# Four KV pairs per round in 32 KB rows, and zero descriptors of 56 KB, in a gradient kernel that writes 280 MB

## The chip, the cores and the metric

The kernel runs on one core of one Trainium2 chip. The metric is the device time of one execution in microseconds (us). The profile is of one execution on the same core; its times start at the span's first instruction.

## The reference, cut to what matters

The kernel computes a gated attention step and its gradients. One token of each of two batches (B = 2) attends to the last W = 4096 positions of a cache of 32768, with 32 query heads on 8 KV heads (4 query heads each) of width 128, all in bfloat16:

```python
q = xn @ wq                        # per head
s = q k_win^T / sqrt(128);  p = softmax(s);  o = p v_win
out = x + (o @ wo) * silu(mlp(xn))
# gradients wanted: x, k_cache, v_cache, wq, wo, w1, b1, w2, b2
dv_win = p^T do;   ds = p * (do v_win^T - delta);   dk_win = ds^T q
```

The gradients of the K and V caches have the caches' full shape, [2, 8, 32768, 128] each. Only the window of 4096 rows of each of the 32 (tensor, batch, head) slabs is not zero. So of 268 MB of cache gradient 235 MB are zeros that have to be written, 33.6 MB are computed, and 33.6 MB of K and V are read.

## The kernel before

**Zero fill.** A tile `zt` of zero bytes (L77) is the source of all zero writes. `zf` (L87 to L94) issues one DMA on the GpSimd queue (q0 in the profile) that reads bytes and writes bfloat16: one byte of `zt` becomes two bytes in memory. With `ZG = 112` rows of 256 bytes a descriptor writes 28 KB, and a slab of 28672 zero rows is 256 descriptors in one DMA. Five slabs are cut by hand (`zshort`) into DMAs of odd shapes. The fills are issued ahead of everything else in program order and run through the whole kernel. The last slab is written at the very end by a DMA on SyncE's queue (L616), which waits for the fill before the last one.

**Prologue.** Small vectors come in on ScalarE's queue (q10): `x`, `grad_out`, `b1`, `b2` (L195 to L201). The weights come in on SyncE's queue (q1): `w1`, `w2`, `wo`, `wq` (L203 to L207). Layernorm, the MLP, q and do are computed; the buffers of this stage lie in a pool `pw` whose memory the attention stage uses again.

**Attention, eight rounds.** A round is one KV head `hk` of both batches. K and V are tiles of 128 partitions by 64 blocks of 128; the even partitions hold batch 0 and the odd ones batch 1, each partition 64 consecutive cache rows (16 KB). A tile is loaded by two DMAs of 1 MB on SyncE's queue (L347) and stored by two on ScalarE's queue (L407). Four tiles of 16 KB per partition rotate (`kvp`, `bufs=4`), so that the next round's loads can be in flight. A round does:

- `scores` of K (L372 transposes, L145/L143 copies out of PSUM, L377 matmuls), then the softmax;
- `scores` of V with do, `contract` of V with p (L392), which gives o, and ds;
- `outer_store` of V: p^T do overwrites the V tile in place (L402 matmuls, copied by ScalarE and VectorE) and is stored;
- `contract` of K with ds, `outer_store` of K, and the round's share of dx and of the gradient of wq (L469 to L485).

The program is written in that order; a planner that works with its own costs and the program's order as priority fixes the order on each engine. On TensorE it puts transposes of the next round's K between the outer products of this round's V.

**Epilogue.** After the rounds the pool's memory goes to the epilogue's tiles. `o_rows` (L496) is the first of them; then come the projection by wo, the MLP's gradients (`dw_st`, stored at L603 and L611), the last zero slab (L616), and the gradient of wo (L621, stored at L623 on ScalarE's queue).

Of the kernel before, what the change touches and what calls it, by code (L numbers as in the profile page):

```python
# [8 lines left out]
ACT = mybir.ActivationFunctionType  # L9
ALU = mybir.AluOpType  # L10
# [6 lines left out]
def kernel(  # L17
# [37 lines left out]
    PB = P // B  # L55
    NCB = W // PB
    CC = NCB // G
    RB = G * REP
    R = B * RB
# [3 lines left out]
    assert B == 2 and REP == 4 and NCB == 64 and DH == P and RB == 32 and CW == 512  # L63
# [12 lines left out]
    ZG = 112  # L76
    zt = const.tile([P, ZG * DH], mybir.dt.uint8, name="zt")  # L77
# [9 lines left out]
    def zf(o, q, r0, nent, rows, rep=1):  # L87
        b, hk = divmod(q, HKV)
        nr = nent * rows * rep
        v = o[b, hk, r0:r0 + nr, :].rearrange("(r p g) d -> p r (g d)", p=nent, g=rows)  # L90
        st = 4 if nent < 16 else 1
        zs = zt[0:nent * st:st, 0:rows * DH].unsqueeze(1).to_broadcast([nent, rep, rows * DH])
        sw_fill.append(nc.gpsimd.dma_start(out=v, in_=zs))  # L93
        return r0 + nr  # L94
# [6 lines left out]
        4: ((3, 1, 2), (2, 99, 6), (128, 112, 1), (128, 102, 1), (86, 1, 1)),  # L101
        6: ((3, 1, 2), (3, 106, 2), (128, 112, 1), (128, 106, 1), (126, 1, 1)),
        8: ((4, 96, 6), (128, 112, 1), (128, 94, 1)),
        10: ((4, 69, 2), (128, 112, 1), (128, 107, 1), (88, 1, 1)),
# [29 lines left out]
    acc_dxn = const.tile([B, D], F32, name="acc_dxn")  # L134
# [35 lines left out]
    nc.vector.tensor_reduce(out=m8[:], in_=ident_bf[0:R, 0:R].rearrange("p (b g i) -> p g b i", b=B, i=REP), axis=AX.XY, op=ALU.add)  # L170
# [6 lines left out]
    NZ = 2  # L177
    ZO = R - REP
    zq_bufs, zdo_bufs, p_bufs = [], [], []
    for j in range(NZ):  # L180
        t = const.tile([P, B, ZO + R], BF16, name=f"zq{j}")
        nc.vector.memset(t[:], 0.0)
        zq_bufs.append(t)
        t = const.tile([P, B, ZO + R], BF16, name=f"zdo{j}")
        nc.vector.memset(t[:], 0.0)
        zdo_bufs.append(t)
        t = const.tile([R, CC, PB, B], BF16, name=f"p{j}")
        nc.vector.memset(t[:], 0.0)
        p_bufs.append(t)
    ds_bf = const.tile([R, CC, PB, B], BF16, name="ds_bf")  # L190
# [137 lines left out]
    kvp = attn.enter_context(tc.tile_pool(name="kvp", bufs=4))  # L328
    kvt = attn.enter_context(tc.tile_pool(name="kvt", bufs=4))
    wsl = attn.enter_context(tc.tile_pool(name="wsl", bufs=1))  # L330
    small = attn.enter_context(tc.tile_pool(name="small", bufs=2))
    hkp = attn.enter_context(tc.tile_pool(name="hkp", bufs=2))
    one = attn.enter_context(tc.tile_pool(name="one", bufs=1))
    bdp = attn.enter_context(tc.tile_pool(name="bdp", bufs=1))

    kwin = slice(SK - W, SK)
    kvs = {}

    def rows_of(t, b, hk):
        return t[b, hk, kwin, :].rearrange("(p c) d -> p c d", c=NCB)  # L340

    def load_kv(hk):
        tiles = []
        for src in (A_k_cache, A_v_cache):
            nat = kvp.tile([P, NCB, DH], BF16, tag="nat")
            for b in range(B):
                dma_load.dma_start(out=nat[b:P:B], in_=rows_of(src, b, hk))  # L347
            tiles.append(nat)
        kvs[hk] = tiles
# [7 lines left out]
    def block_diag(hT, tag):  # L357
        zr = small.tile([P, B, G, REP], BF16, tag="zr" + tag)
        for b in range(B):
            nc.vector.tensor_copy(out=zr[:, b], in_=hT[:, :, b].unsqueeze(1).to_broadcast([P, G, REP]))  # L360
        rp = ps_m.tile([R, P], F32, tag="m")
        nc.tensor.matmul(rp[:], lhsT=zr[:].rearrange("p b g i -> p (b g i)"), rhs=ident_bf[:, :], start=True, stop=True)  # L362
        bd = bdp.tile([R, G, DH], BF16, tag="bd" + tag)
        nc.vector.tensor_tensor(out=bd[:], in0=rp[:].unsqueeze(1).to_broadcast([R, G, DH]),  # L364
                                in1=m8[:].unsqueeze(2).to_broadcast([R, G, DH]), op=ALU.mult)
        return bd

    def scores(out_ps, nat, zbuf):
        for g in range(G):
            tp = ps_t.tile([P, CC, P], BF16, tag="pt")  # L370
            for j in range(CC):
                nc.tensor.transpose(tp[:, j, :], nat[:, g * CC + j, :], ident_bf[:, :])  # L372
            tT = kvt.tile([P, CC, PB, B], BF16, tag="tT")
            evac(tT[:].rearrange("p c k b -> p (c k b)"), tp[:].rearrange("p c k -> p (c k)"), eng=("act" if g % 4 == 3 else "dve"))
            for b in range(B):
                o = ZO - (b * RB + REP * g)
                nc.tensor.matmul(out_ps[:], lhsT=zbuf[:, b, o:o + R], rhs=tT[:, :, :, b],  # L377
                                 start=(g == 0 and b == 0), stop=(g == G - 1 and b == B - 1))

    def col_form(src, tag):  # L380
        tp = ps_m.tile([P, CC, R], BF16, tag="m")
        for cc in range(CC):
            nc.tensor.transpose(tp[:, cc, :], src[:, cc].rearrange("r k b -> r (k b)"), ident_bf[0:R, 0:R])
        t = one.tile([P, CC, B, G, REP], BF16, tag="colT")
        nc.vector.tensor_copy(out=t[:].rearrange("p c b g i -> p c (b g i)"), in_=tp[:])  # L385
        return t

    def contract(nat, tT):
        ps = ps_m.tile([P, B, REP], F32, tag="m")
        for c in range(NCB):  # L390
            g, cc = divmod(c, CC)
            nc.tensor.matmul(ps[:], lhsT=nat[:, c, :], rhs=tT[:, cc, :, g, :],  # L392
                             start=(c == 0), stop=(c == NCB - 1))
        return ps

    def outer_store(src, bd, nat, dst, hk):
# [9 lines left out]
        for b in range(B):  # L406
            dma_store.dma_start(out=rows_of(dst, b, hk), in_=nat[b:P:B])  # L407

    load_kv(0)
    for hk in range(HKV):  # L410
        if hk + 1 < HKV:
            load_kv(hk + 1)
        knat, vnat = kvs.pop(hk)
        hs = slice(hk * REP, (hk + 1) * REP)
        zq, zdo, p_bf = (t[hk % NZ] for t in (zq_bufs, zdo_bufs, p_bufs))
        nc.vector.tensor_copy(out=zq[:, :, ZO:ZO + REP], in_=qT_all[:, hs, :].rearrange("p i b -> p b i"))
        nc.vector.tensor_copy(out=zdo[:, :, ZO:ZO + REP], in_=doT_all[:, hs, :].rearrange("p i b -> p b i"))
        dqT_bf = hkp.tile([P, REP, B], BF16, tag="dqT_bf")
# [15 lines left out]
        for b in range(B):  # L434
            rb = slice(b * RB, (b + 1) * RB)
            nc.scalar.activation(out=p_bf[rb, :, :, b], in_=e_sb[rb], func=ACT.Copy, scale=rl[rb, 0:1])
# [3 lines left out]
        pT = col_form(p_bf, "pT")  # L440
        o_ps = contract(vnat, pT)
        nc.vector.tensor_copy(out=oT_all[:, hs, :].rearrange("p i b -> p b i"), in_=o_ps[:])

        junk = one.tile([R, CC, PB], BF16, tag="junk")
        dpp = small.tile([R, 1], F32, tag="dpp")
        dp_c = dp_ps[:].rearrange("r (c k) -> r c k", c=CC)
        nc.vector.scalar_tensor_tensor(out=junk[:], in0=dp_c, scalar=rl[:, 0:1], in1=e_sb[:],
# [3 lines left out]
        for b in range(B):  # L451
            rb = slice(b * RB, (b + 1) * RB)
            nc.vector.scalar_tensor_tensor(out=ds_bf[rb, :, :, b], in0=dp_c[rb], scalar=delta[rb, 0:1], in1=p_bf[rb, :, :, b],
                                           op0=ALU.subtract, op1=ALU.mult)
        bddo = block_diag(doT_all[:, hs, :], "do")
        outer_store(p_bf, bddo, vnat, out_3, hk)
        dsT = col_form(ds_bf, "dsT")
        dq_ps = contract(knat, dsT)
        nc.scalar.mul(out=dqT_bf[:].rearrange("p i b -> p b i"), in_=dq_ps[:], mul=SCALE)
        bdq = block_diag(qT_all[:, hs, :], "q")  # L460
        outer_store(ds_bf, bdq, knat, out_2, hk)

        wqT = wsl.tile([P, REP, DK, P], BF16, tag="wqT")
        for half in range(2):
            tp = ps_t.tile([P, 8, P], BF16, tag="pt")
            for jj in range(8):
                i, k = divmod(half * 8 + jj, DK)
                n0 = (hk * REP + i) * DH
                nc.tensor.transpose(tp[:, jj, :], wq[:, k, n0:n0 + DH], ident_bf[:, :])  # L469
            evac(wqT[:, half * 2:(half + 1) * 2, :, :].rearrange("q i k p -> q (i k p)"), tp[:].rearrange("q a p -> q (a p)"))  # L470
        xps = ps_m.tile([B, DK, P], F32, tag="m")
        for i in range(REP):
            nc.tensor.matmul(xps[:], lhsT=dqT_bf[:, i, :], rhs=wqT[:, i, :, :], start=(i == 0), stop=(i == REP - 1))
        if hk == 0:
# [4 lines left out]
        for i in range(REP):  # L479
            nc.tensor.transpose(tp[:, i, :], dqT_bf[:, i, :], ident_bf[:, :])  # L480
# [170 lines left out]
```

## Time and profile before

| | |
|---|---|
| median of 3 runs | 769.88 us (769.7 to 770.0) |
| the profiled execution: its own time, and its span | 769.5 us, 767.7 us |
| TensorE matmul, VectorE, ScalarE busy | 468.0, 283.4, 212.0 us |
| moved by the DMA queues | 326.68 MB, mean 426 GB/s |
| of it by q0 (GpSimd: fills), q1 (SyncE), q10 (ScalarE) | 227.55, 56.63, 41.95 MB |
| DMA packets | 17016, of which 3109 under 512 B |

The page has the span in 40 slices of 19.2 us. A line "DMA" gives the busy share of the 16 DMA engines in tenths, a line "GB/s" what they moved. A DMA answer for a stretch of time gives for each queue the packets, the MB and the time that its packets took as a share of 16 engines. In a timeline the bracket at the end of a line is the time for which the engine sat idle before, and what it waited for.

### The profile page before, as it was taken

What the parts mean: (1) busy time and instruction counts of PE and PEld (TensorE: products, weight loads), DVE (VectorE), ACT (ScalarE), POOL (GpSimd) and SP (SyncE); (2) the same over time, 40 slices, a digit from 0 to 9 for tenths busy, and PEclk for the clock granted to TensorE, in tenths of its full rate; (3) what the DMA queues carried; (4) which work ended last, traced back from release to release, by engine and by line L of the source; (5) the groups of instructions that cost most, each with busy time, mean ns of one, the idle gap of its engine ahead of it and who ended that gap; (6) DMA issues with size and microseconds to landing.
All of it is one profiled execution on the core that took longest, in us unless ns stands there. A gap on an engine that the chain in (4) does not pass through costs nothing.

```text
span 767.7 us, 8822 instructions
## 1 busy us (share of the span) xinstructions
PE 468.0 (61%) x3778; PEld 233.6 (30%) x3778; DVE 283.4 (37%) x546; ACT 212.0 (28%) x325; POOL 31.9 (4%) x55
## 2 busy tenths in 40 slices
PE   0166752898498498479569749959884266850000
PEld 0153341444244234233324413433441234210000
DVE  3033331465255255245325415434553034740000
ACT  0034440345135135224324313323442100530000
POOL 3000001010000010000000000000000000000000
PEclk9997885979859759758857955675985565555555
DMA  9999999999999999999999999999999999999998
GB/s 358 432 431 421 437 430 426 427 429 428 431 426 429 427 430 426 431 431 423 429 434 429 424 433 429 425 434 426 428 432 430 432 429 433 429 428 436 432 429 348
DMA packets 17016, 326.68 MB, mean 426 GB/s; under 512 B 3109, under 2 KB 3118, under 8 KB 3128
## 3 DMA queue, kind: packets, MB, share of 16 engines
q0 software_dynamic: 9728, 227.55, 70.0%
q1 hardware_dynamic: 4106, 56.63, 18.0%
q10 hardware_dynamic: 3144, 41.95, 13.2%
q8 instruction: 29, 0.48, 0.2%
q14 instruction: 9, 0.07, 0.0%
HBM read 45.62 MB, written 280.50 MB: 425 GB/s over the span
## 4 chain that ended last, share of the span: by engine, by line
DMA 39%; PE 36%; DVE 7%; ACT 4%; issue 3%; ACTq 0%; SPq 0%; DVEq 0%
DMA nat<-in_A_k_cache_dram 20%; DMA out_dram<-nat 15%; PE ov L402 9%; PE tp L372 6%; DMA b_bf<-in_B_b_dram 4%; PE s_ps L377 3%; PE ps L392 2%; PE wps L621 2%; PE dops L286 1%; PE sps L505 1%; PE tp L282 1%; PE dp_ps L377 1%; DVE dhB_rows L596 1%; PE qps L298 1%; DVE tT L145 1%
## 5 line engine op out<-in xcount | busy, mean ns | idle before, releaser
L372 PE MATMUL tp<-ident_bf,nat 128*128 128x128 bf16 x1024 | 108.2, 252 | 89.2 <-DMA nat<-in_A_k_cache_dram 68.7
L143 ACT CAST nat<-ov 128x512 bf16<-128x512 f32 x160 | 89.8, 588 | 168.9 <-PE ov L402 167.4
L372 PEld LDWEIGHTS <-nat 128*128 128x128 bf16 x1024 | 71.5, 111 | 173.2 <-issue 172.0
L145 DVE COPY tT<-tp 128x1024 bf16<-128x1024 bf16 x96 | 64.6, 682 | 136.7 <-PE tp L372 136.7
L145 DVE CAST nat<-ov 128x512 bf16<-128x512 f32 x96 | 65.4, 688 | 64.1 <-PE ov L402 63.7
L93 POOL DMA_DIRECT2D out_dram<-zt x47 | 30.8, 659 | 543.6 <-DMA out_dram<-zt 540.3
L143 ACT COPY tT<-tp 128x1024 bf16<-128x1024 bf16 x32 | 32.4, 1013 | 74.4 <-PE tp L372 74.2
L402 PE MATMUL ov<-bd,ds_bf 64*128 64x512 bf16 x128 | 50.4, 476 | 1.4 <-DVE bd L364 1.3
L392 PEld LDWEIGHTS <-nat 128*128 128x128 bf16 x1024 | 28.8, 100 | 7.3 <-DVE nat L145 5.0
L392 PE MATMUL ps<-t,nat 128*128 128x8 bf16 x1024 | 30.3, 167 | 0.5 <-DVE t L385 0.5
L377 PE MATMUL s_ps<-tT,zq_164 128*64 128x512 bf16 x64 | 28.6, 514 | 1.7 <-DVE tT L145 1.5
L402 PE MATMUL ov<-bd,p_168 64*128 64x512 bf16 x64 | 28.2, 519 | 2.2 <-ACT nat L143 1.2
L402 PE MATMUL ov<-bd,p_174 64*128 64x512 bf16 x64 | 28.5, 518 | 1.4 <-ACT nat L143 1.2
L377 PE MATMUL s_ps<-tT,zq_170 128*64 128x512 bf16 x64 | 27.5, 488 | 1.0 <-DVE tT L145 0.9
L377 PE MATMUL dp_ps<-tT,zdo_166 128*64 128x512 bf16 x64 | 20.8, 405 | 6.9 <-DVE tT L145 6.0
L377 PE MATMUL dp_ps<-tT,zdo_172 128*64 128x512 bf16 x64 | 19.9, 391 | 7.0 <-DVE tT L145 5.6
L364 DVE TENSOR_TENSOR bd<-rp,m_156 64x1024 bf16<-64x1024 f32 x16 | 19.5, 1216 | 11.7 <-PE rp L362 11.7
L143 ACT CAST dw_st<-wps 128x512 bf16<-128x512 f32 x15 | 8.8, 585 | 48.5 <-PE wps L601 45.7
L402 PEld LDWEIGHTS <-ds_bf 64*128 64x128 bf16 x128 | 10.9, 103 | 25.9 <-issue 22.7
L286 PE MATMUL dops<-woT,dsT_bf 128*2 128x512 bf16 x32 | 10.6, 466 | 12.5 <-ACT woT L143 7.8
L151 PE MATMUL pp<-xT_f,ones_f 128*128 128x2 f32 x8 | 1.9, 355 | 25.6 <-DVE goT L216 25.6
L496 PE MATMUL tp<-ident_bf,oT_all 128*2 128x128 bf16 x32 | 3.6, 263 | 22.6 <-DVE o_rows L145 22.6
(214 smaller groups left out, 510.9 us busy)
## 6 DMA issues: line engine op xcount, KB each, us to landing
out_dram<-zt POOLq DMA_DIRECT2D x26, 7168.0 KB, 176.4
out_dram<-nat ACTq DMA_DIRECT2D x32, 1024.0 KB, 22.3
nat<-in_A_k_cache_dram SPq DMA_DIRECT2D x16, 1024.0 KB, 41.5
nat<-in_A_v_cache_dram SPq DMA_DIRECT2D x16, 1024.0 KB, 20.2
out_dram<-zt POOLq DMA_DIRECT2D x4, 3584.0 KB, 63.4
out_dram<-zt SPq DMA_DIRECT2D x1, 7168.0 KB
out_dram<-zt POOLq DMA_DIRECT2D x1, 5040.0 KB, 73.2
wo<-in_A_wo_dram SPq DMA_DIRECT2D x1, 4096.0 KB, 37.0
```

The lines of the kernel that those rows point to most:

```text
L93: sw_fill.append(nc.gpsimd.dma_start(out=v, in_=zs))
L143: nc.scalar.copy(out=out_ap, in_=in_ap)
L145: nc.vector.tensor_copy(out=out_ap, in_=in_ap)
L282: nc.tensor.transpose(tp[:, jj, :], wo[:, j0 + j, dk:D:DK], ident_bf[:, :])
L286: nc.tensor.matmul(dops[0:B, :, :], lhsT=dsT_bf[:, dk, :], rhs=woT[:, :, dk, :], start=(dk == 0), stop=(dk == DK - 1))
L298: nc.tensor.matmul(qps[0:B, :], lhsT=xnT[:, k, :], rhs=wq[:, k, n0:n0 + 512], start=(k == 0), stop=(k == DK - 1))
L364: nc.vector.tensor_tensor(out=bd[:], in0=rp[:].unsqueeze(1).to_broadcast([R, G, DH]), in1=m8[:].unsqueeze(2).to_broadcast([R, G, DH]), op= ...
L372: nc.tensor.transpose(tp[:, j, :], nat[:, g * CC + j, :], ident_bf[:, :])
L377: nc.tensor.matmul(out_ps[:], lhsT=zbuf[:, b, o:o + R], rhs=tT[:, :, :, b], start=(g == 0 and b == 0), stop=(g == G - 1 and b == B - 1))
L392: nc.tensor.matmul(ps[:], lhsT=nat[:, c, :], rhs=tT[:, cc, :, g, :], start=(c == 0), stop=(c == NCB - 1))
L402: nc.tensor.matmul(ov[:], lhsT=src[:, cc].rearrange("r k b -> r (k b)"), rhs=bd[:, gh * 4:(gh + 1) * 4, :], start=True, stop=True)
L621: nc.tensor.matmul(wps[:], lhsT=o_rows[:, j:N:NJ], rhs=ds_rows[:, :], start=True, stop=True)
```

## The change

The attention stage now takes two KV heads at once, four rounds in place of eight. A tile of K or V holds four (head, batch) pairs: pair `pr` lies on partitions pr, pr+4, pr+8 and so on, each with 128 consecutive cache rows (32 KB). A tile is loaded and stored by four DMAs of 1 MB, each of 32 rows of 32 KB. There is one K tile and one V tile (`bufs=1`, two tags) in the memory that four tiles had. The next round's K is loaded after this round's K gradient is stored, and V likewise. K's gradient now comes ahead of V's in the program. Score matmuls have 256 columns and 128 output rows in place of 512 and 64. The round's share of dx is gathered transposed (`dxqT`), which drops four transposes from the epilogue.

The zero tile keeps its bytes, but one byte now becomes four: `ZG = 224`, and a descriptor writes 56 KB. A slab is 128 descriptors. The last slab on SyncE's queue is written as before.

```diff
-    PB = P // B
+    HH = 2
+    NP = HH * B
+    PB = P // NP
...
-    ZG = 112
-    zt = const.tile([P, ZG * DH], mybir.dt.uint8, name="zt")
+    ZG = 224
+    zt = const.tile([P, ZG * DH // 2], mybir.dt.uint8, name="zt")
...
-        v = o[b, hk, r0:r0 + nr, :].rearrange("(r p g) d -> p r (g d)", p=nent, g=rows)
+        v = o[b, hk, r0:r0 + nr, :].bitcast(F32).rearrange("(r p g) d -> p r (g d)", p=nent, g=rows)
...
-        8: ((4, 96, 6), (128, 112, 1), (128, 94, 1)),
+        8: ((4, 96, 6), (128, 206, 1)),
...
-    kvp = attn.enter_context(tc.tile_pool(name="kvp", bufs=4))
-    kvt = attn.enter_context(tc.tile_pool(name="kvt", bufs=4))
+    kvp = attn.enter_context(tc.tile_pool(name="kvp", bufs=1))
+    kvt = attn.enter_context(tc.tile_pool(name="kvt", bufs=3))
...
+    def pairs(r):
+        return [(hh * B + b, b, r * HH + hh) for hh in range(HH) for b in range(B)]
+
+    def load(src, r, tag):
+        nat = kvp.tile([P, NCB, DH], BF16, tag=tag)
+        for pr, b, h in pairs(r):
+            dma_load.dma_start(out=nat[pr:P:NP], in_=rows_of(src, b, h))
+        return nat
...
-        for b in range(B):
-            dma_store.dma_start(out=rows_of(dst, b, hk), in_=nat[b:P:B])
...
+        for pr, b, h in pairs(r):
+            dma_store.dma_start(out=rows_of(dst, b, h), in_=nat[pr:P:NP])
+
+    NR = HKV // HH
+    knat = load(A_k_cache, 0, "k")
+    vnat = load(A_v_cache, 0, "v")
+    for r in range(NR):
...
         s_ps = ps_s.tile([R, CW], F32, tag="sd")
         scores(s_ps, knat, zq)
...
         dp_ps = ps_s.tile([R, CW], F32, tag="sd")
         scores(dp_ps, vnat, zdo)
...
+        dq_ps = contract(ds_bf, knat)
...
+        bdq = block_diag(qT_all[:, hs, :])
+        outer_store(ds_bf, bdq, knat, out_2, r)
+        if r + 1 < NR:
+            knat = load(A_k_cache, r + 1, "k")
+
+        o_ps = contract(p_bf, vnat)
...
+        bddo = block_diag(doT_all[:, hs, :])
+        outer_store(p_bf, bddo, vnat, out_3, r)
+        if r + 1 < NR:
+            vnat = load(A_v_cache, r + 1, "v")
...
+            xps = ps_m.tile([P, DK, B], F32, tag="m")
+            for k in range(DK):
+                for i in range(REP):
+                    nc.tensor.matmul(xps[:, k, :], lhsT=wqT[:, i, k, :], rhs=dqT_bf[:, hh, i, :], start=(i == 0), stop=(i == REP - 1))
...
-    tp = ps_m.tile([P, DK, B], F32, tag="m")
-    for k in range(DK):
-        nc.tensor.transpose(tp[:, k, :], acc_dxn[:, k * P:(k + 1) * P], ident_f[0:B, 0:B])
-    nc.vector.tensor_tensor(out=dxnT[:], in0=dxnT[:], in1=tp[:], op=ALU.add)
+    nc.vector.tensor_tensor(out=dxnT[:], in0=dxnT[:], in1=dxqT[:], op=ALU.add)
...
-    v = out_3[b, hk, 0:ZR, :].rearrange("(r p g) d -> p r (g d)", p=P, g=ZG // 2)
-    zs = zt[:].bitcast(BF16).unsqueeze(1).to_broadcast([P, 2 * ZR // (P * ZG), ZG * DH // 2])
+    v = out_3[b, hk, 0:ZR, :].rearrange("(r p g) d -> p r (g d)", p=P, g=ZG // 4)
+    zs = zt[:].bitcast(BF16).unsqueeze(1).to_broadcast([P, 4 * ZR // (P * ZG), ZG * DH // 4])
```

## The prediction

> **What bounds the kernel now.** I read the page's slices first, then the queues, then the chain of waits, then the DMA queues in short stretches.
>
> ```profile
> DMA  9999999999999999999999999999999999999998
> GB/s 358 432 431 421 437 430 426 427 429 428 431 426 429 427 430 426 431 431 423 429 434 429 424 433 429 425 434 426 428 432 430 432 429 433 429 428 436 432 429 348
> ...
> q0 software_dynamic: 9728, 227.55, 70.0%
> q1 hardware_dynamic: 4106, 56.63, 18.0%
> q10 hardware_dynamic: 3144, 41.95, 13.2%
> ```
>
> The DMA engines are full in every slice but the first and the last. From 20 to 760 us they move 317.66 MB at 429 GB/s in 16242 packets. TensorE, the busiest other engine, works 61% of the span. So the kernel is bound by DMA traffic, and the zero fills (q0) are what fills every gap that the attention rounds leave. The bytes don't change, so a gain can only come from the rate. A loss comes if the rounds end so late that the fills no longer cover them. How late the rounds end now is in three timelines, of ScalarE, its queue, and SyncE's queue:
>
> ```profile
> 607.39 1.00 ACT L143 COPY o_rows<-tp 2x1024 bf16<-2x1024 bf16 x1 [21.29 <-DMA out_dram<-nat]
> ...
> 682.41 0.35 ACTq L623 DMA_DIRECT2D out_dram<-wo  x1
> ```
> ```profile
> 731.89 0.39 SPq L616 DMA_DIRECT2D out_dram<-zt  x1
> ```
>
> The last gradient tile has left at 607, the epilogue's last store is issued 75 us later at 682, and it lands after 25.7 us, at about 708. The fills last to the end: the last slab's DMA (L616) waits until 732 for the fill before the last. So the chain through the rounds has some **60 us of slack**.
>
> How long a round takes is seen in the chain of waits and in ScalarE's queue:
>
> ```profile
> 305.08 0.47 SPq L347
> ...
> 305.60 23.92 DMA nat<-in_A_k_cache_dram
> ...
> 329.65 0.59 PE tp L372 x4
> ```
> ```profile
> 282.06 1.14 ACTq L407 DMA_DIRECT2D out_dram<-nat  x2
> ...
> 295.46 1.14 ACTq L407 DMA_DIRECT2D out_dram<-nat  x2
> ...
> 343.33 1.14 ACTq L407 DMA_DIRECT2D out_dram<-nat  x2
> ```
>
> V's store is issued at 282.1; SyncE waits for it until 305.1 (23 us for 2.1 MB), loads the next K (24 us), TensorE finishes the held outer products, and the next V store goes at 343.3. That is a period of 61 us per KV head, of which 47 are two transfers in a row. A transfer is slow because it shares the engines with the fills. The queues from 24 to 28 us, 229 to 237 and 213 to 221:
>
> ```profile
> q1 hardware_dynamic: 32, 1.05, 61.5%
> q0 software_dynamic: 24, 0.69, 40.3%
> q10 hardware_dynamic: 24, 0.00, 0.3%
> ```
> ```profile
> q0 software_dynamic: 85, 2.36, 69.2%
> q10 hardware_dynamic: 75, 1.08, 32.7%
> ```
> ```profile
> q0 software_dynamic: 91, 2.06, 61.0%
> q1 hardware_dynamic: 93, 1.26, 38.0%
> ```
>
> The queues take turns by packet: 24 fills and 24 tiny vector packets in the first, 85 to 75 and 91 to 93 in the others. A store beside the fills gets 1.08 MB in 8 us (135 GB/s), a load 1.26 MB (157 GB/s).
>
> [...]
>
> **The change, part by part.**
>
> *Fewer packets.* Fills of 56 KB drop 227.5 MB / 28.7 KB / 2 = about 3970 packets, rows of 32 KB drop 67.1 MB / 16.4 KB / 2 = 2050. [...] This is the whole possible gain, and it counts only if the fills still cover the rounds. The cast to four bytes isn't in the trace. That it writes at the same rate is my assumption [...]; [...] a slower one is a rival below. I take 0 here, since the path computed below ends later than the fills.
>
> *Turns.* A 32 KB row beside a 56 KB fill has the same share as 16 beside 28, so a transfer's rate stays. A tile is now 4.2 MB, so each transfer doubles. The wait for the first packet is 5 to 6 us now (load issued at 109, first packets of q1 after 115), which fits some five fill packets already queued on an engine (1.05 us each). With packets twice as long I take 8 (5 to 10).
>
> *Prologue.* The vectors take about 11 turns on each engine while fills run (177 fill packets from 8 to 32 us / 16). Each turn gets 1.05 us longer: +11.5 us (0 to 15), and the chain of waits begins with these vectors (30.76 us for `b_bf`). `wo` and `wq` land later too (8 and 16 turns behind, about 53 and 80), but are needed at 49 + 11.5 and 88 + 11.5. The first K load moves from 108.6 to 120. Its tile and V's are 8.4 MB at about 165 GB/s, 51 us, plus 8: **V complete at 179**.
>
> *A round of four pairs.* Compute is mostly unchanged in sum: as many transposes and copies, score columns (64 x 256 for 2 x 16 x 512 per tile) and outer products. What changes is what it may lie beside. With single tiles, from V's landing to its successor's:
>
> 1. V's landing to the K store's issue: V scores of 128 blocks 20 us (64 take 10: 144.3 to 154.3); delta and ds 5 (0.73 + 0.4 + 4 x 0.78); two column copies and transposes 3; contract 3.7 (64 matmuls 1.8); block diagonal 2.4; 32 outer products 16 (16 take 7.3 to 10.4). About **51** (45 to 60).
> 2. K store beside the fills: 8 + 4.2 MB / 135 GB/s 31 [...] = **41**. SyncE's K load waits for it, and V's load is queued behind that. Under this lie V's contract and outer products (22 us); V's store joins the same queue behind K's.
> 3. K load beside the rest of V's store: 8 us to the first packet, then three queues (16/60 of 430 = 115 GB/s each) until V's store is out, then 157 GB/s: about **43**.
> 4. V load, already queued: 4.2 MB / 160 = **26**; K's scores and softmax of the new round (24 + 8 us) lie under it.
>
> The sum is about **160 us** for two KV heads, where before it is 2 x 61 = 122. The double buffer is what is lost: V's scores, K's outer products, a store and two loads now stand in a row.
>
> *End.* V lands for the last round at 179 + 3 x 160 = 659. Fills by then: up to 179 us 75.6 MB moved less 20.5 of loads = 55; each period 160 x 0.43 - 16.8 = 52; together 211 of 227.5 MB. The rest takes 38 us: **the fills end near 697 and the engines fall idle**. K's last store is issued at 659 + 51 = 710 [...], V's lands near 746. The epilogue starts when the pool's memory is free: 724 if `o_rows` waits for K's tile, 746 if for both; I take 735. Then 75 us as now to its last store (810), with the last slab (7.3 MB, issued 61 us in, behind the 3.6 MB of `dw_st`) and the 4.2 MB of `wo` left, 23 to 31 us: about 833. The four transposes saved are 1 us.
>
> The profiled execution is 769.5 (span 767.7 and 1.8 around it; the median is 0.4 above). Against it: the epilogue starts at 735 for 607, +128, which is 120 (first load) + 59 (V complete) + 480 (three periods) + 51 (compute) + 25 (last stores). The slack takes up 768 - 708 = 60 of it, and the last transfers take some 3 us less than the 25.7 of now. 769.5 + 128 - 60 - 3 gives **835**.
>
> **The rivals.**
>
> - *A (56%): as above*, 790 to 885 by the ends of the terms (compute 6 to 9 us either way in four rounds, transfers 10 in three, prologue).
> - *B (24%): TensorE's order holds V's outer products behind the next K.* Now the planner does so: TensorE starts three outer products of V at 257.0 and then idles 10.6 us in front of the next K's transposes. With one K tile that wait is a whole store and load. Then V's store, and V's load behind it, follow K's load: 51 + 41 + 36 + 20 + 41 + 36 = 225 per period, the last ones quicker since the fills are out by 655: about 912. Against it: V's outer products are only 22 us of work, and K's transfer longer than that by any planner's cost.
> - *C (14%), the other side: the fills still cover the rounds.* Then only the packets count[...]. It needs the rounds to end 70 us earlier than I have it, a period of at most 137. That would be so if the engines cut a 56 KB fill into pieces of 28 KB: then a 32 KB row gets 53% of a turn, the transfers shrink from 110 to about 83 us, and the period is 134. Against it: 32 KB rows of `wo` go unsplit now (32 packets, 1.05 MB).
> - *D (6%): a one-to-four cast is slower [...].* [...]
>
> **How the numbers follow.** The likeliest is A with 835. The range takes in A, most of B and the upper part between A and C: 780 to 920; left out are C below (14%) and D above (6%). Since A and B lie on one side, no range of A's own is wanted beyond the 790 to 885 above. A measurement of this kernel tells a change of about 0.2% from none. Faster: C's better part, 0.11. Same: the rest of C, 0.03. Slower: A, B, D, 0.86.
>
> **What would show it.** Right: q0's packets down to about 5800, fill packets of 57 KB, 32 KB rows one for one with them; `b_bf` near 42 us in place of 30.8; K's store to K's load about 40 us apart; a DMA row that falls below 9 after about 700 with rates under 430; the chain's end in the epilogue. Wrong: a DMA row full to the end, or a period under 137 us.

## The result, and the profile after

The changed kernel takes **914.02 us** (median of 6 runs, 911.57 to 915.25); the kernel before took 769.94 beside it. The ratio is 1.187, 95% interval 1.1846 to 1.1885. The profiled execution took 913.59 us, its span 911.2. The forecast was 835 (780 to 920): the direction and the range hold, but only 65 of the 144 us of loss were foreseen.

The page of the kernel after, slices of 22.8 us and the queues:

```profile
DMA  9999999999999999999999999999858400453069
GB/s 369 447 409 443 430 428 433 438 426 436 431 432 435 429 438 419 436 441 431 429 429 424 440 439 423 435 433 429 345 204 350 186 1 1 186 219 151 1 282 386
DMA packets 11067, 326.73 MB, mean 359 GB/s; under 512 B 3045, under 2 KB 3054, under 8 KB 3064
...
q0 software_dynamic: 5824, 227.55, 58.9%
q1 hardware_dynamic: 3082, 56.63, 20.2%
q10 hardware_dynamic: 2120, 41.95, 12.9%
```

The packets fell by 5950, and the rate while fills run is about the same (432 GB/s from 20 to 640 us, for 429 before), so the fills themselves are no slower. But they are out at 658 us, and then the DMA engines wait for the rounds: the slack of 60 us is gone and the bound has changed sides. The rounds, first in the issues of K's stores and the epilogue's start (ScalarE and its queue), then in the issues of K's and V's loads (SyncE's queue), both of the kernel after:

```profile
253.77 2.47 ACTq L410 DMA_DIRECT2D out_dram<-nat  x4
...
464.26 2.42 ACTq L410 DMA_DIRECT2D out_dram<-nat  x4
...
668.03 3.94 ACTq L410 DMA_DIRECT2D out_dram<-nat  x4
...
787.19 3.94 ACTq L410 DMA_DIRECT2D out_dram<-nat  x4
...
817.90 1.00 ACT L148 COPY o_rows<-tp 2x1024 bf16<-2x1024 bf16 x1 [5.91 <-DMA out_dram<-nat]
```
```profile
120.72 2.44 SPq L344 DMA_DIRECT2D nat<-in_A_k_cache_dram  x4
...
300.68 2.57 SPq L344 DMA_DIRECT2D nat<-in_A_k_cache_dram  x4
338.82 2.62 SPq L344 DMA_DIRECT2D nat<-in_A_v_cache_dram  x4
511.17 2.55 SPq L344 DMA_DIRECT2D nat<-in_A_k_cache_dram  x4
```

From K's store to the next K's store is 210.5, 203.8 and, with the fills out, 119.2 us. The forecast had 160 three times. The epilogue starts at 817.9 in place of 735, and from there the kernel ends about as forecast (93 us to the end of the span, for 100). Where TensorE waits in the second round, and for V's landing in the third, is in its timeline (the bracket is idle time before the line):

```profile
350.85 1.87 PE L372 MATMUL tp<-ident_bf,nat 128*128 128x128 bf16 x16 [76.01 <-DMA nat<-in_A_k_cache_dram]
...
389.85 1.87 PE L372 MATMUL tp<-ident_bf,nat 128*128 128x128 bf16 x16 [10.35 <-DMA nat<-in_A_v_cache_dram]
...
441.25 0.39 PE L394 MATMUL ps<-t,nat 128*128 128x16 bf16 x9 [8.82 <-issue]
...
604.75 1.55 PE L372 MATMUL tp<-ident_bf,nat 128*128 128x128 bf16 x13 [14.66 <-DMA nat<-in_A_v_cache_dram]
```

The first line is the serial chain that the forecast described: K's store, then K's load, with TensorE idle for 76 us. The other three are waits that its sum did not hold. Two tables of packets show what went on ahead of them. From 438 to 440 us, ahead of the wait that ends at 441.25:

```profile
q0 software_dynamic: 16, 0.92, 109.0%
q8 instruction: 1, 0.02, 3.1%
```

The wait has no releaser ("issue"), and it ends 1.3 us after one 16 KB packet of q8 (439.0 to 440.0), a queue whose kind the trace gives as "instruction". So do all five waits of this kind in the gradient part of the three rounds beside fills: they are 3.8 to 8.8 us long, and each ends 1.3 to 1.4 us after a packet of q8. What the packets hold, and why TensorE stands still ahead of them, is not shown. From 589 to 589.5 us, ahead of 604.75:

```profile
q1 hardware_dynamic: 4, 0.03, 571.7%
q0 software_dynamic: 3, 0.17, 80.8%
```

The share is packet time over 16 engines: 5.717 x 16 x 0.5 us = 45.7 us for four packets. One is V's last 32 KB (1.26 us). The other three are four-byte packets: 14.8 us each, where such a packet otherwise takes 2.3 us or less in the rounds. They end at 604.1 to 604.3, the last of V's landings in the trace is at 604.62, and TensorE goes on at 604.75. V's last data packet had ended at 590.6. Ahead of 389.85 one such packet took 8.6 us. In the whole trace a landing follows the end of a four-byte packet by 0.2 us (median of 1918); the expectations of e13 and e14 call them completion packets.

### The profile page after: what moved, and what is told of

Same layout as the page of the kernel before. It is cut to its first block, busy times and chain, and to the rows that moved or that the text cites. A ratio compares the mean times of both kernels' runs of the same rounds, so it can differ in the third digit from the quotient of the medians.

```text
span 911.2 us, 9484 instructions
## 1 busy us (share of the span) xinstructions
PE 462.3 (51%) x4118; PEld 278.8 (31%) x4118; DVE 279.1 (31%) x495; ACT 214.1 (24%) x317; POOL 25.1 (3%) x51
## 4 chain that ended last, share of the span: by engine, by line
DMA 36%; PE 34%; DVE 11%; ACT 7%; issue 6%; ACTq 2%; another core or an unknown queue 2%; SPq 1%; DVEq 0%
DMA out_dram<-nat 15%; DMA nat<-in_A_k_cache_dram 11%; PE dp_ps L378 6%; DMA nat<-in_A_v_cache_dram 5%; PE s_ps L378 5%; DMA b_bf<-in_B_b_dram 5%; PE ov L405 4%; PE tp L372 4%; DVE tT L150 3%; PE ps L394 3%; ACT nat L148 2%; DVE ds_bf L450 2%; PE wps L629 2%; ACTq L410 1%
## 5 line engine op out<-in xcount | busy, mean ns | idle before, releaser
L372 PE MATMUL tp<-ident_bf,nat 128*128 128x128 bf16 x1024 | 87.0, 238 | 221.8 <-DMA nat<-in_A_k_cache_dram 195.5
L378 PE MATMUL dp_ps<-tT,zdo 128*128 128x256 bf16 x256 | 67.3, 403 | 16.6 <-DVE tT L150 13.4
L378 PE MATMUL s_ps<-tT,zq 128*128 128x256 bf16 x256 | 66.3, 403 | 13.6 <-ACT tT L148 7.4
L405 PE MATMUL ov<-bd,p_bf 128*128 128x512 bf16 x128 | 48.8, 456 | 13.7 <-DVE bd L362 6.6
L394 PE MATMUL ps<-t,nat 128*128 128x16 bf16 x1024 | 36.3, 174 | 28.5 <-issue 28.5
L405 PE MATMUL ov<-bd,ds_bf 128*128 128x512 bf16 x128 | 49.5, 444 | 1.0
L378 PEld LDWEIGHTS <-zdo 128*128 128x128 bf16 x256 | 27.5, 111 | 36.3 <-issue 20.0
L378 PEld LDWEIGHTS <-zq 128*128 128x128 bf16 x256 | 27.6, 111 | 34.5 <-issue 16.9
L438 ACT ACTIVATE p_bf<-e_sb,rl 32x512 bf16<-32x512 f32 x16 | 22.9, 1432 | 3.7 <-DVE rl L435 3.5
L450 DVE SCALAR_TENSOR_TENSOR ds_bf<-dp_ps,delta,p_bf 32x512 bf16<-32x512 f32 x16 | 21.5, 1346 | 0.3
```

What stands on the lines that cost most here:

```text
L372: nc.tensor.transpose(tp[:, j, :], nat[:, g * CC + half * CH + j, :], ident_bf[:, :])
L378: nc.tensor.matmul(out_ps[:, half * CH * PB:(half + 1) * CH * PB], lhsT=zbuf[:, pr, o:o + R], rhs=tT[:, :, :, pr], start=(g == 0 and pr == ...
L394: nc.tensor.matmul(ps[:], lhsT=nat[:, g * CC + half * CH + cc, :], rhs=cols[half][:, cc, :, g, :], start=(half == 0 and g == 0 and cc == 0 ...
L405: nc.tensor.matmul(ov[:], lhsT=src[:, cc].rearrange("r k b -> r (k b)"), rhs=bd[:, gh * 4:(gh + 1) * 4, :], start=True, stop=True)
L438: nc.scalar.activation(out=p_bf[rb, :, :, pr], in_=e_sb[rb], func=ACT.Copy, scale=rl[rb, 0:1])
L450: nc.vector.scalar_tensor_tensor(out=ds_bf[rb, :, :, pr], in0=dp_c[rb], scalar=delta[rb, 0:1], in1=p_bf[rb, :, :, pr], op0=ALU.subtract, o ...
```

## The experiments

Two theories at the start. **W**: the wide fills (56 KB, one byte cast to four) slow everything that shares the engines. **S**: the serial four-pair round, with one tile of each kind, is what costs.

**e1: the change with the old fills** (28 KB, one byte to two).

```diff
-    ZG = 224
+    ZG = 112
...
-        v = o[...].bitcast(F32).rearrange(...)
+        v = o[...].rearrange(...)
...
```

> The four-pair rounds with the fills of before (28 KB, one byte to two). Theory W (the 56 KB fill packets make each transfer wait longer for its first packet, for its completion and for each turn[...]): waits of 10 and 8 us fall to about half, a 32 KB row beside a 28 KB fill gets 53% of a turn (230 GB/s alone), so a period falls from 199 to 215 us to about 140, the rounds end near 680, and the time is 765 to 790. TensorE's gaps of 6 to 9 us marked as issue fall to 3 to 5. Theory S (single tiles: a store and two loads in a row, whatever the fills' size): the period stays above 180 and the time above 870.

Measured: 816.12 us, ratio to before 1.060 (1.0585 to 1.0621). It lies between the two, so neither holds alone. The period is 154 us, near the 160 that the prediction had for the new fills.

**e2: the kernel before with the new fills.**

```diff
-    ZG = 112
+    ZG = 224
...
-        v = o[...].rearrange(...)
+        v = o[...].bitcast(F32).rearrange(...)
...
```

> The eight rounds of before with fills of 56 KB (one byte to four). Theory W: a 16 KB row beside a 56 KB fill gets 22% of a turn (96 GB/s), and each wait doubles, so a store and a load take 40 us each for 23 and 24, the period per KV head goes from 61 to about 95, the rounds end near 770 and the time is 830 to 870. Theory S: double buffers are kept, so the time is 765 to 785.

Measured: 866.62 us, ratio 1.126 (1.1241 to 1.1275), the period of one KV head 88 us where it was 61. The wide fills alone cost 97 us, in a kernel whose double buffer is whole.

**e3 and e4: the change and the kernel before with no fills.**

```diff
-    for qi in range(ZQ - 1):
-        ...
-        fin = nc.sync.dma_start(out=v, in_=zs)
```

> The changed kernel with all zero fills left out (the zero rows are not written): the chain alone. Theory W: transfers at the full rate take 12 to 14 us for 4.2 MB, the prologue is some 25 us shorter, a period is about 55 + 13 + 13 + 13 = 95 to 105 (the last one under idle engines took about 135 with part of it still beside fills), and the time is 480 to 540; no issue gap over 2 us in the outer products. Theory S: the period is above 130 without any fill, time above 600.

> The kernel before with all zero fills left out: its chain alone. Both theories: the rounds become bound by TensorE and the copies, 35 to 42 us per KV head, time 430 to 490. The difference to the changed kernel without fills is what the single tiles cost by themselves: by W 20 to 80 us, by S over 130.

Measured: 667.61 and 564.35 us, one run each. The 564 lies above what both theories expected, since the compute of a round is longer than either had it. The 667 lies in S's range of time, but the period of 117 us for two KV heads lies between the two theories, and so do the 103 us between the runs. The kernel before has a period of 88 us, so the four-pair round loses 29 us even on a free DMA system. K's stores in e3, on ScalarE's queue:

```profile
195.35 4.00 ACTq L404 DMA_DIRECT2D out_dram<-nat  x4
...
311.93 3.96 ACTq L404 DMA_DIRECT2D out_dram<-nat  x4
```

K's load is issued at 208.13, 12.8 us after the store, and TensorE takes up the next K at 223.92, 28.6 us after the store, and from there to the next store it is 88 us of compute in a row. So the 29 us are K's store and load, which nothing covers any more. With runs of e9 and e12 below, the times stand so:

| fills | none | 28 KB, 1 to 2 | 28 KB, 1 to 4 | 56 KB, 1 to 4 |
|---|---|---|---|---|
| two pairs (before) | 564.4 | 769.9 | 785.3 | 866.6 |
| four pairs (after) | 667.6 | 816.1 | 880.4 | 914.0 |

At the old fills the structure costs 46 us, at the new ones 47; the fills cost 97 and 98. **The two parts add up** to the 144. This is no rule of the times: without fills the structure costs 103 us, and at 28 KB one to four 95, since the time also depends on how much of a longer round the fills still cover (60 us of slack at the old fills). What does add up everywhere is the period of two KV heads while fills run: 88, 122, 140 and 175 us in the kernel before, 117, 154, 174 and 207 in the four-pair kernel, 29 to 34 us more in each column.

**e5 and e6: both kernels with fills of 14 KB** (one byte to two; e5 on top of e1's edit, the hand-cut slabs as before), to see whether packet length goes on mattering.

```diff
-        for n, rows, rep in zshort.get(qi, ((P, ZG, ZR // (P * ZG)),)):
+        for n, rows, rep in zshort.get(qi, ((P, ZG // 2, 2 * ZR // (P * ZG)),)):
```

> The four-pair rounds with fill packets of 14 KB (one byte to two, 56 rows). Theory W (waits and turns scale with the fill packet): K store to K landed falls from 97 us (56 KB) and 59 (28 KB) towards the 28 without fills, about 42; the period from 207 and 155 to about 132; the rounds end near 645, under the cover of the fills again, and the time is that of the DMA traffic: 771 to 774 [...]. Rival (a fixed cost per transfer beside any fill, not the packet's length): period stays near 150, time above 800.

> The kernel before with fill packets of 14 KB: it is bound by DMA traffic, so the 7900 packets more are all that changes in its time. [...] If packets cost nothing, 769.9. The rounds end earlier than 607 by W (period 61 towards 50).

Measured: the four-pair kernel 784.25 (ratio 1.019, 1.0174 to 1.0205; period 144 in place of 154), the kernel before 771.12 (1.0015, 1.0009 to 1.0022; per head about 55 in place of 61). e5 misses both of its expectations (W's 771 to 774, the rival's 800 and more). Shorter packets do make the rounds quicker, but before gains nothing by it, since its fills cover them. It has 6656 packets more and takes 1.15 us longer. If all of that is theirs, it is an estimated 1.15 x 16 / 6656 = **2.8 ns per packet** (1.7 to 4.1 by the interval). So the 5950 packets that the change saves were worth an estimated 1.0 us.

**e7: the kernel before with one K and one V tile** in place of four.

```diff
-    kvp = attn.enter_context(tc.tile_pool(name="kvp", bufs=4))
+    kvp = attn.enter_context(tc.tile_pool(name="kvp", bufs=1))
...
+    knat = load(A_k_cache, 0, "k")
+    vnat = load(A_v_cache, 0, "v")
...
+        if hk + 1 < HKV:
+            vnat = load(A_v_cache, hk + 1, "v")
...
+        if hk + 1 < HKV:
+            knat = load(A_k_cache, hk + 1, "k")
```

> The eight rounds and 28 KB fills of before with one K tile and one V tile of 16 KB, each reloaded only after its store (the change's order of loads, nothing else of it). Theory S (the lost double buffer costs by itself: a store and a load stand in the chain with both scores behind them): per head 23 + 24 of transfers and 50 of compute, about 97 to 105 for 61; the fills run out near 675; time 880 to 930. If the change's other parts (256-column score matmuls, strided p and ds) are what costs, the time stays under 800.

Measured: 906.07 us (one run) and 97.5 per head, as expected. With the old fills, the loss of the double buffer takes two heads from 122 to 195 us. The four-pair round (e1) has 154, which fits that it pays for the chain of store and load half as often.

**e8: before, with wide packets only after the rounds.** It asks whether a long packet costs anything where nobody waits beside it.

```diff
+        g = 2 * ZG
+        v = o[b, hk, 0:ZR, :].bitcast(F32).rearrange("(p g) d -> p (g d)", g=g)
+        sw_fill.append(nc.gpsimd.dma_start(out=v, in_=zt[:]))
...
+        if qi >= 25:
+            zf_wide(*zparts[qi])
+            continue
```

> The kernel before with 56 KB fills (one byte to four) for the last six slabs only, which run after the rounds: nothing waits behind them but the epilogue's stores. [...] 769.4 to 769.8, not told apart from before. If it is slower by over 2 us, long packets also cost where no chain waits for a transfer.

Measured: 769.68, ratio 0.9997 (0.9989 to 1.0005). It costs nothing there: the first wide packet starts at 625 us, and the last gradient tile has landed at 609.

**e9: before with 28 KB packets, but cast one to four.** Up to here length and cast ratio had gone together.

```diff
-        v = o[...].rearrange("(r p g) d -> p r (g d)", p=nent, g=rows)
+        v = o[...].bitcast(F32).rearrange("(r p g) d -> p r (g d)", p=nent, g=rows)
...
-        zs = zt[0:nent * st:st, 0:rows * DH]...
+        zs = zt[0:nent * st:st, 0:rows * DH // 2]...
```

> The kernel before with its 28 KB fill packets kept and only the cast changed, one byte to four (7 KB read for 28 KB written). If the length of the fill packets is what slows the rounds, the time is that of before, 769.5 to 770.5, with the rounds ending near 607. If the wider cast itself is slow or takes more of the engines, the time goes towards the 866 of the eight rounds with 56 KB fills.

Measured: 785.27, ratio 1.021 (1.0192 to 1.0226), between the two expectations; the period of one head is 70 us, 9 above before, and 18 more come with the length (e2, 88). The length alone does not explain the wide fills. A new theory, **R**: the wait of a transfer for its first packet goes with the fills' cast ratio. It was some 6 us at one to two (before) and 11 at one to four (e9). If all but 1.5 us of it goes with the ratio (4.5 and 9.5), uncast fills leave about 4, an estimate from these two waits.

**e10 and e11: 14 KB fills without a cast**, in the kernel before and in the four-pair kernel.

```diff
-            zs = zt[0:nent * st:st, 0:rows * DH]...
+            zs = zt[:].bitcast(BF16)[0:nent * st:st, 0:rows * DH]...
...
+            if rows > ZG // 2:
+                r = zf(*zparts[qi], r, n, rows // 2, 2 * rep)
```

> The kernel before with fills of 14 KB that aren't cast (14 KB read for 14 KB written). Theory R [...]: the first packet of a load comes 4 us after its issue, for 6 with the cast to two and 11 with the cast to four; the period is a little under the 55 us of 14 KB with the cast to two. Theory L (the packet's length alone sets the wait): 6 us as with the other 14 KB packets. The time is that of the DMA traffic in both, about 771 to 773.

> The four-pair rounds with fills of 14 KB that aren't cast. Theory R: each of the three or four waits of a period is some 2 us shorter than with 14 KB cast to two, so the period falls from 143 to about 135, the epilogue starts near 665 for 688, and the time is 772 to 778 for 784. Theory L: 784 as before.

Measured: 808.18 (one run) and 806.82 (1.050, 1.0448 to 1.0547), 35 and 29 us above the upper ends of what was expected, where cast fills of 14 KB took 771 and 784 (e6, e5). In e10 the rounds end earlier than before (o_rows at 551 for 607), so the fills are what is late. From 20 to 110 us its queues moved 377 GB/s, and from 130 to 600 they moved 421, where the kernel before has 429:

```profile
q0 software_dynamic: 10171, 132.33, 67.6%
q10 hardware_dynamic: 2704, 37.75, 19.0%
q1 hardware_dynamic: 2250, 27.36, 13.7%
```

(e10, 130 to 600 us; before has 138.00 MB of q0 in 5674 packets there.) So the times of these two runs are no clean test of R at ratio one; their waits are in the table below. Why uncast fills run slower is open.

**e12: the change with 28 KB packets, cast one to four.**

```diff
-    ZG = 224
-    zt = const.tile([P, ZG * DH // 2], mybir.dt.uint8, name="zt")
+    ZG = 112
+    zt = const.tile([P, ZG * DH], mybir.dt.uint8, name="zt")
...
```

> The four-pair rounds with fills of 28 KB made by the cast of one byte to four. Theory R: waits of 11 us at every transfer as in the changed kernel, turns as in the 28 KB fills: period about 172 (154 at one to two, 207 with 56 KB), time 840 to 870. Theory L: 816, as with 28 KB cast to two.

Measured: 880.36, ratio 1.143 (1.1411 to 1.1449). Of the 98 us that the wide fills cost the four-pair kernel, 64 come from the cast ratio at equal length (816 to 880), and 34 from the length. That is the split of the time, in which the ratio counts for much already before the first K store (23 us later in e12 than in e1), and the length gets some back in the last period, which in after has no fills beside it (119 us for 161 in e12). In the full periods it is the other way round: 154, 174 and 207 us, 20 for the ratio and 33 for the length, as in the kernel before (61, 70 and 88 per head). K's store shows what each does. It takes 28 to 30 us in e1, 36 in e12 and 47 in after. Of this the wait for the first packet is 6.5, 11.5 and 11.8, and the transfer 21 to 24, 24 and 35. The ratio lengthens the wait, the length mainly the transfer, through the turns. The wait of the first K load shows the ratio's part. In e12 the load is issued at 110.36; its queues from 111 to 120, and those of e1 (issued at 107.96) from 114 to 115:

```profile
q0 software_dynamic: 248, 3.87, 106.0%
q8 instruction: 1, 0.02, 0.7%
```
```profile
q1 hardware_dynamic: 10, 0.33, 76.9%
q0 software_dynamic: 7, 0.19, 43.7%
```

In e1 the load's q1 has its packets after 6 us; in e12 it has none for ten. From the issue to the first data packet, in us, in the four-pair kernels (e3, e11, e5, e1, e12, after), stores and loads of the rounds only where fills still run:

| fills | none | 14 KB uncast | 14 KB, 1:2 | 28 KB, 1:2 | 28 KB, 1:4 | 56 KB, 1:4 |
|---|---|---|---|---|---|---|
| first K load | 1.3 | 5.1 | 6.4 | 6.5 | 10.9 | 11.8 |
| K's stores | 1.1 to 1.2 | 3.9 to 4.4 | 6.4 to 6.6 | 6.4 to 6.6 | 11.0 to 11.8 | 11.7 to 11.9 |
| K's loads in the rounds | 1.3 | 3.7 to 5.9 | 4.9 to 5.1 | 4.1 to 5.5 | 5.5 to 6.4 | 8.4 |

Where only fills are under way at the issue, as at the first K load and K's stores, the wait follows the ratio and hardly the length. K's loads in the rounds start beside V's store, and there the length counts too. R came out in direction, though its time was at least 10 us too low.

**e13 and e14: a small load behind V's**, to see whether V's four-byte packets are late because nothing stands behind them on the queue; e14 is the same on e1, where no four-byte packet took over 6.7 us.

```diff
-            dma_load.dma_start(out=nat[pr:P:NP], in_=rows_of(src, b, h))
+            ld = dma_load.dma_start(out=nat[pr:P:NP], in_=rows_of(src, b, h))
+        if tag == "v":
+            tail = one.tile([P, 4, DH], BF16, tag="tail")
+            with tc.issue_after(ld.ins):
+                dma_load.dma_start(out=tail[:], in_=src[0, 0, 0:512, :]...)
```

> The kernel after, with one more small load (128 rows of 1 KB, 0.13 MB, into a tile that nothing reads) right behind each V load on SyncE's queue; all else is the same. In the kernel after, V's last data packets were through by about 381 and 590 us, but its last four-byte completion packets took 8.6, 12.8 and 14.8 us, and TensorE's first V transposes followed at 389.85 and 604.75. H (a queue that runs empty beside fills that cast one byte to four gets its last completion late): with work behind V on its queue V's completions come in turn, so that V's landing follows K's by 28 to 31 us in place of 39.0 and 43.6, the periods are about 200 and 190 us in place of 210.5 and 203.7, and the time is 885 to 902. T (the four extra microseconds of rate in both rounds and a late reading of the landing, no held completion): the landings stay at 39 and 43, and the time is 912 to 918, a little longer for the added packets.

> The same small load behind each V load, in the four-pair kernel with fills of 28 KB that cast one byte to two (816.1 us). There no completion packet took over 6.7 us. H: nothing is held, so nothing is gained: 815.5 to 818.5. If the small load helped for another reason than the held completion (an order on SyncE's queue, an earlier start), it would help here too: under 812.

Measured: 905.21 (ratio to before 1.176, 1.1739 to 1.1781, below the 1.1846 to 1.1885 of after) and 818.21 (1.062, 1.0604 to 1.064; e1 had 1.060). TensorE's first V transposes in e13:

```profile
383.49 1.89 PE L376 MATMUL tp<-ident_bf,nat 128*128 128x128 bf16 x16 [3.60 <-DMA nat<-in_A_v_cache_dram]
...
587.50 1.87 PE L376 MATMUL tp<-ident_bf,nat 128*128 128x128 bf16 x16 [4.51 <-issue]
```

They follow K's landing by 32.7 and 33.2 us, for 39.0 and 43.6 in the kernel after. In the third round the four-byte packets that take up to 8.5 us are now those of the small load, at 599 us, for which nobody waits. H holds in kind, and the control gains nothing. The small load gave 9 us, 3 short of the expected range, because the two gains of 8 us per period are partly returned in the last one (123.5 for 119.2), which the fills now reach into.

No version beat the kernel before; e8 equals it.

## Why the prediction was right in direction and short in size

**Right.** The DMA rate stays (432 for 429), so a one-to-four cast is not slower as a stream, and the fills do take 57 KB each: D is out. The packets are worth an estimated 1 us (from e6), and the forecast took 0 for them. The prologue lands as forecast (the DMA of `b_bf` takes 44.25 us for 42, the first K load is issued at 120.7 for 120), as do the epilogue's 75 us (74) and the idle engines at the end. The chain of V's scores, K's store, K's load and V's load is the one that sets the period. C did not come: a 56 KB fill goes as one packet (3328 of 57344 bytes).

**Right time, wrong mechanism: B's 912.** TensorE does not hold V's outer products behind the next K. It had started the last of them at 267 us and then idled 76 us in front of the next K (first line of its timeline above). That B's number is the measured one is chance, and the range took in 914 only because it was drawn to take in B.

**Wrong: the terms of A's sum.** The path was right. Each of its four steps was mis-sized, by a term taken too small or left at nothing. A landing is counted here by TensorE's first transposes of the tile, a store by its issue.

| step | forecast | 2nd round | 3rd round | what was missed |
|---|---|---|---|---|
| V's landing to K's store | 51 | 74.4 | 63.3 | waits without a releaser, score matmuls |
| K's store | 41 | 46.9 | 46.9 | first-packet wait |
| K's load | 43 | 50.2 | 50.0 | transfer beside V's store |
| V's load after K's | 26 | 39.0 | 43.6 | late four-byte packets |

1. *The wait for a first packet, taken as 8 (5 to 10).* K's stores wait 11.9 and 11.7 us (253.77 to 265.69, and 464.26 to 475.94). The prediction read the 5 to 6 us of before as five packets already queued. Packets of twice the length would then give 10 to 12, and it took 8 without a reason. The reading itself is wrong too: at one to four, packets of 28 KB wait as long as those of 56 (the table by cast ratio). K's loads in the rounds do wait 8.4, so that step's 7 us lie in the transfer.
2. *The time from a transfer's last data to its landing, taken as nothing for V's load.* The 41 us for K's store hold 2 for it, which no trace had shown: in before the next load is issued 0.7 us after the last packet of a V store (304.42 to 305.08). Beside one-to-four fills some four-byte packets take over 8 us: 20 of the 645 on q1 in after, 52 in e12 and 41 in e9. The 20 in after all belong to a load with nothing queued behind it, 15 of them to the weights' in the prologue. Beside one-to-two fills there are none in before and e1, and a single one in each of e5, e6 and e7. V's load is the last on its queue, so this stood on the path with 8.6 and 14.8 us. In e13, with a load behind it, V's landing followed K's 6 and 10 us sooner.
3. *The compute, 51.* Two errors. V's scores take 27 us for the 20 that were doubled from a tile of before, and no less in e3, so the fills are not what it comes from. The prediction set 64 matmuls of 256 columns equal to 32 of 512. The timelines of before and of after, from the start of a group of score matmuls to the next group's:

```profile
144.33 0.61 PE L377 MATMUL dp_ps<-tT,zdo_166 128*64 128x512 bf16 x2 [2.37 <-DVE tT L145]
144.87 0.40 PE L372 MATMUL tp<-ident_bf,nat 128*128 128x128 bf16 x4
```
```profile
189.79 1.07 PE L378 MATMUL dp_ps<-tT,zdo 128*128 128x256 bf16 x4
190.69 0.46 PE L372 MATMUL tp<-ident_bf,nat 128*128 128x128 bf16 x5
```

   Two in 0.54 us, 0.27 each; four in 0.90, 0.225 each. 64 x 0.225 less 32 x 0.27 is 5.8 us more per tile. The ds operations, with bfloat16 at every fourth element in place of every second, take 1.346 us for 0.776, 2.3 us a round. Second, TensorE's waits without a releaser. In this stretch they sum to 9.9, 16.0 and 6.4 us in three rounds. From the ds transposes to K's store TensorE took 33.9, 40.7 and 29.6 us. Less the waits that is 24.0, 24.7 and 23.2, against some 25 forecast (3 + 3.7 + 2.4 + 16); without fills (e3) it is about 22. So scores, ds and these waits make up the step's excess.
4. *The fills' end, 697.* With longer periods the fills are out at 658, and the last period is 119 in place of 160. This pays 41 us back. So 50 + 44 - 41 = 53 us more in three periods, 4 at the first V (landed at 177 for 179, but TensorE was still at K's scores and took V up at 182.5), 20 in the first compute and 6 at the end make the 83 us by which the epilogue is late.

The turns themselves went by packet as forecast. From 351 to 361 us 48 fill packets of 57 KB (2.75 MB) stand beside 47 of V's of 32 KB (1.54 MB). They alternate: from 340 to 372 us a fill starts within 6 ns of the end of 105 of the load queue's 121 data packets, and another packet of that queue, but no fill, at 10. From 361 to 381 it is 112 beside 65; why is not shown.

R stands between one to two and one to four: 6.5 us to the first packet in e1, 10.9 to 11.8 in e12 and after. At 4 to 5 us the uncast wait (e11) does not fall to half of the 6.5, as one in proportion to the ratio would. What makes the wait follow the ratio is open. So is why some four-byte packets in e9 and e12 took 4 to 7 us and others 15, and why K's loads in the rounds of after wait 3.4 us less than K's first.

## What to carry to other kernels

The background DMA stream cost its neighbours here by its turns and by latency. Price such a stream by the share of the engines that its packets leave to a transfer (K's store took 21 to 24 us of transfer beside 28 KB packets and 35 beside 56), and by each wait on the path that got longer beside it: for a first packet (6.4 to 11.9 us at K's stores beside cast fills, 1.1 to 1.2 without fills), for late four-byte packets (up to 14.8), and TensorE's without a releaser (up to 8.8); and count how often a round passes one. For a stream that fills gaps, try short packets and the narrower cast first: its own gain from longer packets was an estimated 1 us here, and wide fills cost the kernel before 97 us (e2). Not casting it at all was slower here (e10 808.18 us for 771.12 in e6, e11 806.82 for 784.25 in e5), so that too is tried alone first. And where one tile takes the place of a rotating pair, take a run of the new round without the background work first: here it would have shown 117 for 88 us, with nothing to be blamed on the DMA engines.

## What the runs showed of the hardware that was not expected

- Where only fills run at the issue, their cast ratio sets how long another queue waits for its first packet: 6.5 us at one byte to two, 11 to 12 at one to four, at 28 KB both (e1, e12), and 1.3 without fills (e3). At 56 KB and one to four it is 11.8 (after).
- Beside one-to-four fills the last four-byte packets of a load take up to 14.8 us, and the last of them ended 13.6 us after the load's last data packet (590.6 to 604.26, after). With a small load queued behind, V's landing came 6 and 10 us sooner, and packets of up to 8.5 us were those of the small load (e13). Beside uncast fills none on q1 took over 0.02 us (e10, e11), as without fills (e3, e4).
- TensorE has waits without a releaser in the gradient part of the rounds. They are 3.8 to 8.8 us each beside 56 KB, one-to-four fills, and end 1.3 to 1.4 us after a 16 KB packet of q8 (after). They are 4.1 to 7.6 us beside 28 KB at one to four (e12); beside 28 KB at one to two the longest of the first round is 1.03 us (e1), and without fills none is over 0.22 us from 200 to 309 us (e3).
- Uncast fills of 14 KB from the GpSimd queue leave the engines at 377 to 421 GB/s where cast ones have 429 (e10, before); the cause is open.
- A score matmul of 256 columns costs 0.225 us where one of 512 costs 0.27, here with weights of 128 columns in place of 64 and with moving columns at every fourth element in place of every second; which of the differences counts was not separated.
